# Blank matmuls before the first values, and an earlier turn of the second batch's z, in a gated attention unit followed by a feed-forward layer

## The chip, the cores and the metric

The kernel runs on one core of one Trainium2 chip. A core has TensorE (PE) for matmuls, VectorE (DVE) and ScalarE (ACT) for elementwise work on what TensorE leaves, GpSimd (POOL) and SyncE (SP). In this kernel SP only issues transfers, in the order of its list; POOL does elementwise work and issues transfers too. The metric is the time of one execution in microseconds on the device, as the median of several runs.

## The reference

Eight batches of 3008 rows. For each batch the scores are z times z transposed, divided by 3008, negative ones set to 0, and squared; they weigh the rows of v, and the result is multiplied elementwise by u. All 24064 rows then go through a feed-forward layer of 2048 hidden values with the gate h * sigmoid(1.702 h).

```python
batch, seq, d_model = (8, 3008, 256); d_qk = 64
scores = (1.0 / S) * np.matmul(z, z.transpose(0, 2, 1))
attn = np.maximum(scores, 0.0) ** 2
x = (u * np.matmul(attn, v)).reshape(B * S, D)
h = x @ w_in                       # 256 -> 2048
g = h * (1.0 / (1.0 + np.exp(-1.702 * h)))
out = g @ w_out                    # 2048 -> 256
```

## The kernel before

**Units.** The rows of a batch are cut into six units of 512 rows (the last is shorter). Unit n is batch n // 6, part n % 6. `scores` computes z times z transposed for a pair of 128-row tiles against the 512 rows of a unit: two matmuls (L263), a relu that leaves the PSUM tile `sc` (ACT, L292, or DVE, L294), and a square in place (ACT L278 or DVE L280). The squares are kept in a ring of 14 tiles `ap_`, or, for units 0 and 1, in memory lent from buffers that the second batch needs only later: the second value buffer V16[1], the second turned z, ZT[1], and z16. Since scores are symmetric, from unit 3 on part of the squares are not computed again but taken transposed by a transfer (L242, tiles `T`).

**Values.** `values` multiplies squares with v (L403; L465 for the last half tile) into four PSUM banks, two for each half h of a unit. `both_sums` moves two banks to a tile `sums` (ACT L382, DVE L384), POOL adds its halves (L377) and multiplies by u (L419) into X. X is transposed by SP (L318, XT), and its row halves are swapped into XS (L336). There are three `sums` buffers, shared with the second layer: the one for the last half of unit 4 is the one that held the first output half of block 0 until its store (L548).

**Feed-forward.** `hidden` computes two groups of 128 hidden values for a block of 512 rows (L493), ACT the sigmoid (L500), DVE the product (L504); `outs` multiplies by w_out (L531) into the same PSUM banks as the values. The block of unit n is worked three units later.

**Order.** The whole program is laid out by a planner at build time: it keeps a clock `now` for each engine with estimated costs, and a list `work` of value and output steps that TensorE takes in order. When a step isn't ready, or a PSUM tile for `sc` or `hg` is free, `filler` may put in a score pair or a hidden group, whichever is more urgent by its due place in `work`. Elementwise work goes to the engine that the planner has free first; SP's transfers are sorted by due unit. The order on each engine is fixed by this, and at run time each engine goes through its own list and waits on semaphores.

**Side steps.** Loads of later data hang on certain places of `work`: `at(n, j, f)` runs f when TensorE's list comes to value tile j of unit n. Each first calls `hold`, a POOL copy of two elements of the newest square, so that POOL (and so the transfers behind it) waits until the program has come that far. For each batch b these places issue `load_z` (POOL, three transfers into z16), `turn_z` (POOL copies z next to itself, L118, then SP transposes all of z16 into ZT, L119, 24 blocks of 128), and four quarters of v (`load_v`, POOL). The first scores of the next batch need ZT; they come in the fifth unit of the batch before.

**Start.** z of batch 0 is loaded in four parts, cast, and turned by TensorE itself (`turn_q`, L634), while eight matmuls on a blank tile run ahead of it (L625). Then come the first scores; the values (L403) begin when the first squares are there.

Of the kernel before, what the change touches and what calls it, by code (L numbers as in the profile page):

```python
# [8 lines left out]
F32 = mybir.dt.float32  # L9
F16 = mybir.dt.float16  # L10
P = 128
# [3 lines left out]
def kernel(  # L15
# [13 lines left out]
    B, S, D = u.shape  # L29
# [15 lines left out]
    LAG = 3  # L45
    RING = (LAG + 1) * TB
    H = P // 2
# [5 lines left out]
    dve, act, pe, sp, pool = nc.vector, nc.scalar, nc.tensor, nc.sync, nc.gpsimd  # L53
# [7 lines left out]
    psB = ctx.enter_context(tc.tile_pool(name="psB", bufs=1, space=bass.MemoryType.PSUM))  # L61
# [21 lines left out]
    def rows(b, dram, lo, hi, dst, eng, twice=2):  # L83

        full = min(hi, NF)
        if full > lo:
            eng.dma_start(  # L87
                dst[:, :full - lo, :],
                dram[b, lo * P:full * P].rearrange("(n p) d -> p n d", p=P),
            )  # L90
        if hi > NF:
            for h in range(twice):
                eng.dma_start(dst[h * SREM:(h + 1) * SREM, NF - lo, :], dram[b, NF * P:S].unsqueeze(1))
# [4 lines left out]
    def load_v(b, q):  # L98
        rows(b, v, q * VN, (q + 1) * VN, V16[b % 2][:, q * VN:(q + 1) * VN, :], pool)
# [5 lines left out]
    def load_z(b):  # L105
        rows(b, z, 0, NJ, z16[:, :, 0, :], pool)
# [9 lines left out]
    def turn_z(b):  # L116
        turned.add(b)
        pool.tensor_copy(z16[:, :, 1, :], z16[:, :, 0, :])  # L118
        sp.dma_start_transpose(ZT[b % 2], z16.rearrange("p n a d -> p (n a d)"))  # L119
# [8 lines left out]
    T_SC, T_SW, T_MM, T_HG = 0.215, 0.1, 0.107, 0.215  # L128
    T_LAT, T_SEM, T_DMA = 0.25, 0.1, 3.5
    now = {"pe": 6.0, "act": 6.0, "dve": 7.0, "pool": 6.0, "sp": 6.0}  # L130
# [21 lines left out]
    def advance(t):  # L152

        while ops:
            best = None
            for o in ops:
                e = min(o[3], key=lambda x: max(now[x], o[0]) + cost[(x, o[2])])
                key = (max(now[e], o[0]), o[2] not in FIRST, o[2] == "sq", o[1])
                if best is None or key < best[0]:
                    best = key, o, e  # L160
            (start, *_), o, e = best
            if start > t:
                break
            ops.remove(o)
            now[e] = start + cost[(e, o[2])]
            o[4](e, now[e] + T_SEM)
        while now["sp"] <= t:
            can = [o for o in sends if o[0] <= t and (o[4] is None or o[4]())]
            if not can:
                break  # L170
            o = min(can, key=lambda o: (o[2], o[0]))
            sends.remove(o)
            now["sp"] = max(now["sp"], o[0]) + cost[("sp", o[1])]
            o[3](now["sp"])

    def pe_at(rows_, dur):
        if mode[0] != rows_:
            now["pe"] += T_SW
            mode[0] = rows_
        now["pe"] += dur  # L180
        return now["pe"] + T_LAT
# [39 lines left out]
    def hold():  # L221

        pool.tensor_copy(scrap, latest[0][:1, 0, :2])
# [140 lines left out]
    def half(x, g):  # L364
        return x[g * H:(g + 1) * H]
# [94 lines left out]
    def halves(n):  # L460

        V = V16[n // NIS % 2]
        for q in range(NIB // 2):
            for g in range(2):
                pe.matmul(  # L465
                    Os[(n, g)][g][:, q, :], half(squares_of(n, NJ - 1, 2 * g + q), g), half(V[:, NJ - 1, :], g),
                    start=False, stop=False,
                )
        pe_at(H, 2 * T_MM)
        drop(n, NJ - 1)  # L470
# [15 lines left out]
    def hidden(m, fg):  # L486
        p_ = take_ps()
        hg = psA.tile([P, 2, TB], F32, name="hg", tag="A")
        p0 = (m * TB) % RING
        for c in range(2 * NK):  # L490
            for e in range(2):
                x = XT if c % 2 == e else XS
                pe.matmul(  # L493
                    hg[:, e, :], half(W1[:, fg // 2, c, fg % 2 * P:(fg % 2 + 1) * P], e), half(x[:, c // 2, p0:p0 + TB], e),
                    start=(c == 0), stop=(c == 2 * NK - 1),
                )

        def sig(e, at):
            tsg = pb.tile([P, 2, TB], F16, name="tsg", tag="tsg")
            act.activation(tsg, hg, AF.Sigmoid, scale=1.702 / FSC)  # L500

            def gt(e, at):
                GT = pb.tile([P, 2, TB], F16, name="GT", tag="GT", bufs=NG)
                dve.tensor_tensor(GT, hg, tsg, ALU.mult)  # L504
                GTs[(m, fg)] = (GT, at)
                set_ps(p_, at)

            push(at, "gt", ("dve",), gt)

        push(pe_at(H, 4 * T_HG), "sig", ("act",), sig)  # L510
# [45 lines left out]
    work = []  # L556
    EDGE, TAIL, NFIRST, NLAST = 6, 9, 4, 4
    for n in range(NTB + LAG):
        m = n - LAG
# [33 lines left out]
    def at(n, j, *fns):  # L593
        def go():
            hold()
            for f in fns:
                f()
        side[(n, j)] = go
# [4 lines left out]
    for b in range(1, B):  # L603
        n0 = (b - 1) * NIS
        late = b == 1
        at(n0 + 1 + 2 * late, 13, lambda b=b: load_z(b))
        at(n0 + 2 + 2 * late, 13, lambda b=b: turn_z(b))
        for q in range(VQ):
            at(n0 + 3 + late + q // 2, (EDGE, 12)[q % 2], lambda b=b, q=q: load_v(b, q))


    NZ = NJ // 4
# [8 lines left out]
    blank = pap.tile([P, 2, ISUP], F16, name="blank", tag="ap_")  # L621
# [9 lines left out]
    def turn_q(q):  # L631
        ztps.append(psB.tile([P, NZ, P], F16, name="ztp", tag=f"B{q % 2}{q // 2}"))
        for jj in range(NZ):
            pe.transpose(ztps[q][:, jj, :], z16[:, q * NZ + jj, :, :].rearrange("p a d -> p (a d)"), ident)  # L634

    def keep_q(q):
        dve.tensor_copy(ZT[0][:, q * NZ:(q + 1) * NZ, :], ztps[q])
# [10 lines left out]
    cast_z(3)  # L648
    keep_q(2)
    turn_q(3)  # L650
    now["pe"] = 8.0
    advance(7.0)
    keep_q(3)

    def ready_of(w):

        if w[0] in "ors":
            at = [squares_at(w[1], j) for j in w[2]] + [v_at[w[2][-1] // VN] if w[1] < NIS else 0.0] + ([bank[w[3]]] if w[0] == "o" and w[2][0] == 0 else [])
        else:
            at = [GTs.get((w[1], w[2]), (None, None))[1]] + ([bank[w[3]]] if w[2] == 0 else [])  # L660
        return None if None in at else max(at)

    def urgent(key, lead):
        return before[due[key]] - before[wi] - lead

    def filler():

        p_ = ps_free[ps_next % 2]
        if p_ is None or p_ > now["pe"]:
            return None  # L670
        can = []
        if nxt < len(pairs) and pairs[nxt][0] // NIS in turned and min(now["act"], now["dve"]) < now["pe"] + 0.8:
            old = len(ring) - NA
            if pairs[nxt] in home or old < 0 or not a_left[ring[old]]:
                can.append((urgent(("a",) + pairs[nxt], 3.0), "a"))
        if hnext < len(hids) and hnext - outs_done < NG and now["act"] < now["pe"] + 1.5 and now["dve"] < now["pe"] + 2.0:
            m = hids[hnext][0]
            xt = xt_at[m * TB // 64:(m + 1) * TB // 64]
            if None not in xt and max(xt) <= now["pe"]:
                can.append((urgent(("h",) + hids[hnext], 5.0), "h"))  # L680
        return min(can, default=None)

    wi = 0
    while wi < len(work):
        advance(now["pe"])
        w = work[wi]
        r = ready_of(w)
        late = r is None or r > now["pe"]
        f = filler()
        if f:  # L690
            if f[1] == "a":
                scores(1)
            else:
                hidden(*hids[hnext])
                hnext += 1
            continue
        if late:
            step = min([t for t in [r, ps_free[ps_next % 2]] + [o[0] for o in ops + sends] + [now[e] for e in ("act", "dve", "pool", "sp")] if t is not None and t > now["pe"]], default=now["pe"] + 0.1)
            now["pe"] = step
            assert now["pe"] < 2000.0  # L700
            continue
        if w[0] == "o":
            key = (w[1], w[2][0])
            if key in side and w[3] == 0:
                side.pop(key)()
            values(*w[1:])
        elif w[0] == "r":
            halves(w[1])
        elif w[0] == "s":
            shorts(w[1])  # L710
        else:
            outs(*w[1:])
        wi += 1
# [34 lines left out]
```

## Time and profile before

| what | us |
|---|---|
| time, median of 3 runs (lowest, highest) | 1249.58 (1248.88, 1251.04) |
| the profiled execution's own time | 1251.23 |
| its span | 1249.33 |
| TensorE busy | 1228.6 |
| DVE busy | 937.6 |
| ACT busy | 819.1 |
| POOL busy | 472.5 |
| HBM read, written | 60.29 MB, 24.64 MB |

The span is the part of an execution between the first and the last instruction that the profiler records; the profiled execution's own time is 1.90 us longer than it. Mean granted clock of TensorE over the span: 0.996 of full speed. Lines of the kernel are given as L and a number; `out<-in` names the tile written and the tiles read. A wait is given with what ended it. The chain is followed back from the last instruction to whatever released each step.

### The profile page before, as it was taken

How to read it: one execution, taken by the hardware profiler on the slowest of the kernel's cores; microseconds unless marked ns; L12 is line 12 of the kernel's file. 1: busy time of each engine (PE TensorE's matmuls, PEld its weight loads, DVE VectorE, ACT ScalarE, POOL GpSimd, SP SyncE). 2: the span in 40 equal slices, each digit the busy share in tenths (PEclk: the TensorE clock that was granted, in tenths of full speed). 3: DMA queues.
4: the chain of work that ended last, by engine and by line, in shares of the span. 5: the costliest groups of instructions: out<-in, count | busy, mean ns of one | idle time of the engine just before them, and what ended most of it. 6: DMA issues, size and time to landing. Idle time of an engine off the chain costs nothing.

```text
span 1249.3 us, 41891 instructions
## 1 busy us (share of the span) xinstructions
PE 1228.6 (98%) x18584; PEld 1011.8 (81%) x18584; DVE 937.6 (75%) x906; ACT 819.1 (66%) x933; POOL 472.5 (38%) x447
## 2 busy tenths in 40 slices
PE   8998999999999999999999999999999999999998
PEld 5876789988998877888778887788877888778886
DVE  7975877777888778876788768877688776877556
ACT  7855676666767657766577656676566765766444
POOL 5443334332433324343343424343343434332331
PEclk8999999999999999999999999999999999999999
DMA  9997887766986939889398684969759877574211
GB/s 151 172 166 153 145 138 131 133 132 123 133 149 135 154 91 143 142 138 165 77 142 155 128 147 90 139 125 166 131 105 141 161 127 119 112 137 110 67 45 60
DMA packets 442135, 161.74 MB, mean 129 GB/s; under 512 B 351841, under 2 KB 441953, under 8 KB 441953
## 3 DMA queue, kind: packets, MB, share of 16 engines
q1 hardware_dynamic: 390528, 141.62, 59.0%
q0 software_dynamic: 51424, 17.44, 13.8%
q8 instruction: 145, 2.38, 0.8%
q14 instruction: 38, 0.30, 0.1%
HBM read 60.29 MB, written 24.64 MB: 68 GB/s over the span
## 4 chain that ended last, share of the span: by engine, by line
PE 93%; DVE 5%; issue 1%; DMA 0%; ACT 0%; DVEq 0%; ACTq 0%
PE O L403 36%; PE hg L493 25%; PE yps L531 24%; PE sc L263 6%; PE O L478 1%; DVE GT L504 1%; PE O L465 1%; DMA ZT<-z 0%; PE warm L625 0%; DVE sums L384 0%; PE ztp L634 0%; DVE ap__8041 L280 0%; DVE ap__2880 L280 0%; DVE ap__713 L280 0%; DVE ap__18581 L280 0%
## 5 line engine op out<-in xcount | busy, mean ns | idle before, releaser
L504 DVE TENSOR_TENSOR GT<-hg,tsg 128x1024 f16<-128x1024 f32 x376 | 456.7, 1220 | 211.1 <-ACT tsg L500 209.9
L500 ACT ACTIVATE tsg<-hg 128x1024 f16<-128x1024 f32 x376 | 380.9, 1023 | 274.8 <-PE hg L493 248.2
L377 POOL TENSOR_TENSOR sums<-sums 128x512 f32<-128x512 f32 x188 | 249.0, 1325 | 666.4 <-ACT sums L382 349.4
L493 PE MATMUL hg<-XT,W 64*128 64x512 f16 x1504 | 387.9, 376 | 3.0 <-DVE GT L504 1.9
L531 PE MATMUL yps<-W,GT 64*128 64x256 f16 x6016 | 374.2, 270 | 1.3 <-DVE GT L504 0.9
L493 PE MATMUL hg<-XS,W 64*128 64x512 f16 x1504 | 370.3, 376 | 0.0
L531 PEld LDWEIGHTS <-GT 64*128 64x128 f16 x6016 | 324.1, 94 | 47.5 <-DVE GT L504 1.4
L493 PEld LDWEIGHTS <-W 64*128 64x128 f16 x3008 | 175.9, 94 | 87.5 <-issue 6.1
L403 PE MATMUL O<-V,T 64*128 64x256 f16 x3392 | 217.4, 269 | 0.1
L403 PEld LDWEIGHTS <-T 64*128 64x128 f16 x3392 | 185.9, 94 | 28.1 <-issue 0.3
L419 POOL TENSOR_TENSOR X<-sums,RU 128x512 f16<-128x512 f32 (+2 forms) x104 | 140.6, 1353 | 7.8
L263 PE MATMUL sc<-ZT 64*128 64x512 f16 x688 | 126.6, 380 | 10.7 <-DMA ZT<-z 4.5
L382 ACT ACTIVATE sums<-O 128x512 f32<-128x512 f32 x114 | 65.2, 596 | 52.8 <-PE O L403 47.1
L384 DVE TENSOR_SCALAR sums<-O 128x512 f32<-128x512 f32 x78 | 52.9, 687 | 33.9 <-PE O L403 30.1
L382 ACT ACTIVATE sums<-yps 128x512 f32<-128x512 f32 x111 | 63.8, 592 | 17.1 <-PE yps L531 15.9
L384 DVE TENSOR_SCALAR sums<-yps 128x512 f32<-128x512 f32 x73 | 50.0, 685 | 14.1 <-issue 9.9
L263 PEld LDWEIGHTS <-ZT 64*128 64x128 f16 x688 | 40.1, 95 | 17.8 <-issue 7.6
L87 POOL DMA_DIRECT2D V<-in_v_dram x32 | 28.0, 878 | 0.0
L87 POOL DMA_DIRECT2D z<-in_z_dram x7 | 10.9, 1564 | 0.4 <-PE hg L493 0.4
L478 PE MATMUL O<-V,T 128*64 128x256 f16 x160 | 10.3, 275 | 0.0
L118 POOL COPY z<-z 128x1536 f16<-128x1536 f16 x7 | 10.2, 1452 | 0.0
L478 PEld LDWEIGHTS <-T 128*64 128x64 f16 x160 | 8.1, 110 | 1.9 <-issue 1.9
(1536 smaller groups left out, 1522.2 us busy)
## 6 DMA issues: line engine op xcount, KB each, us to landing
out_dram<-sums SPq DMA_DIRECT2D x92, 256.0 KB, 4.0
RU<-in_u_dram SPq DMA_DIRECT2D x40, 512.0 KB, 4.5
V<-in_v_dram POOLq DMA_DIRECT2D x24, 384.0 KB, 7.2
XS<-XT SPq DMA_DIRECT2D x60, 128.0 KB, 4.0
RU<-in_u_dram SPq DMA_DIRECT2D x8, 384.0 KB, 3.7
z<-in_z_dram POOLq DMA_DIRECT2D x7, 368.0 KB, 9.4
V<-in_v_dram POOLq DMA_DIRECT2D x8, 320.0 KB, 9.1
XT<-X SPq DMA_TRANSPOSE x144, 2.5
```

Source lines behind the costliest of these rows:

```text
L87: eng.dma_start(dst[:, :full - lo, :], dram[b, lo * P:full * P].rearrange("(n p) d -> p n d", p=P),)
L263: pe.matmul(sc[:, g, :], Z[h0:h0 + DQK, 2 * t + g, :], Z[h0:h0 + DQK, isup * NIB:(isup + 1) * NIB, :], start=True, stop=True,)
L377: pool.tensor_tensor(s_[:, 0, :, :], s_[:, 0, :, :], s_[:, 1, :, :], ALU.add)
L382: act.activation(s_[:, g, :, :], ps[g], AF.Copy, scale=scale)
L384: dve.tensor_scalar(s_[:, g, :, :], ps[g], scale, None, ALU.mult)
L403: pe.matmul(O[g][:, i2, :], half(sq, g), half(V[:, j, :], g), start=(j == 0 and i2 == 0), stop=(ends and j == js[-1] and (i2 == 1 or short)),)
L419: pool.tensor_tensor(X[:p, :, ib:ib + k, :].rearrange("p c n d -> p n c d"), both[:p, ib - 2 * h:ib - 2 * h + k, :].rearrange("p n (c d) - ...
L478: pe.matmul(O[c0:c0 + SREM, 1, :], squares_of(n, j, NIB - 1)[:, :SREM], V[:, j, :], start=False, stop=False, tile_position=(0, c0),)
L493: pe.matmul(hg[:, e, :], half(W1[:, fg // 2, c, fg % 2 * P:(fg % 2 + 1) * P], e), half(x[:, c // 2, p0:p0 + TB], e), start=(c == 0), stop= ...
L500: act.activation(tsg, hg, AF.Sigmoid, scale=1.702 / FSC)
L504: dve.tensor_tensor(GT, hg, tsg, ALU.mult)
L531: pe.matmul(Y[g][:, i2, :], half(GT[:, e, s * P:(s + 1) * P], g), half(W2[:, ff, :], g), start=(fg == 0 and e == 0 and i2 == 0), stop=(end ...
```

## The change

Three things are edited. First, while the planner has not yet placed the first value step (`wi == 0`) and finds TensorE waiting, it puts in matmuls of 64 rows by 256 columns on the blank tile, into a PSUM tile `idle` that nothing reads. Second, for the second batch alone, `load_z` hangs on value tile 8 of the fourth unit instead of 13, `turn_z` on tile 0 of the fifth unit instead of 13, and the first `load_v` of each pair on tile 7 instead of 6. Third, `filler` gets a condition for the hidden groups of block 0.

```diff
-        at(n0 + 1 + 2 * late, 13, lambda b=b: load_z(b))
-        at(n0 + 2 + 2 * late, 13, lambda b=b: turn_z(b))
+        at(n0 + 1 + 2 * late, 8 if late else 13, lambda b=b: load_z(b))
+        at(n0 + 2 + 2 * late, 0 if late else 13, lambda b=b: turn_z(b))
         for q in range(VQ):
-            at(n0 + 3 + late + q // 2, (EDGE, 12)[q % 2], lambda b=b, q=q: load_v(b, q))
+            at(n0 + 3 + late + q // 2, (EDGE + late, 12)[q % 2], lambda b=b, q=q: load_v(b, q))
...
     turn_q(3)
+    idle = psB.tile([P, D], F32, name="idle", tag="B00")
     now["pe"] = 8.0
...
-            if None not in xt and max(xt) <= now["pe"]:
+            if None not in xt and max(xt) <= now["pe"] and (m or work[wi][1] >= LAG or work[wi][0] == "y"):
                 can.append((urgent(("h",) + hids[hnext], 5.0), "h"))
...
             step = min([t for t in [r, ps_free[ps_next % 2]] + [o[0] for o in ops + sends] + [now[e] for e in ("act", "dve", "pool", "sp")] if t is not None and t > now["pe"]], default=now["pe"] + 0.1)
+            if wi == 0 and step - now["pe"] > 0.08:
+
+                pe.matmul(idle, half(blank[:, 0, :P], 0), half(blank[:, 0, :D], 0), start=True, stop=True)
+                pe_at(H, T_MM)
+                continue
             now["pe"] = step
```

In the lists of instructions that the two programs give, TensorE's differs by 16 blank matmuls with their weight loads, and DVE's and ACT's are the same. On POOL the doubling copy of z (L118) with its `hold` stands ahead of two quarter loads of v instead of behind them, and the `hold` ahead of the z load names an earlier square. On SP the transpose into ZT (L119) stands ahead of two stores (L548) and two swaps (L336) instead of behind them, directly behind the transpose of the square that the trace of before calls ap__1501.

## The prediction

> **What bounds the kernel now.** I read the page first (shares, chain), then TensorE's waits, then the stretches around the two largest waits, then SP's timeline. On the page:
>
> ```profile
> PE 1228.6 (98%) x18584; PEld 1011.8 (81%) x18584; DVE 937.6 (75%) x906; ACT 819.1 (66%) x933; POOL 472.5 (38%) x447
> PE 93%; DVE 5%; issue 1%; DMA 0%; ACT 0%; DVEq 0%; ACTq 0%
> ```
>
> TensorE is busy 98% of the span and carries 93% of the chain. Its instruction list after the change is the old one with 16 matmuls added, so time can be won only where TensorE waits or runs slowly. Its waits (us in total, times, longest):
>
> ```profile
> PE sc L263 <- DMA ZT<-z: 4.5, 1, 4.5
> ...
> PE sc L263 <- DVE ap__181 L294: 1.1, 1, 1.1
> ...
> PE sc L263 <- DVE ap__150 L294: 0.9, 1, 0.9
> ...
> PE sc L263 <- ACT ap__176 L292: 0.3, 1, 0.3
> ```
>
> One wait of 4.5 us stands out: scores that need the second batch's turned z. The other three lie at the start. Stretches (bounds, length, busy time of PE, PEld, DVE, ACT, POOL; then granted clock, DMA share, GB/s):
>
> ```profile
> 7.00:10.00 3.00, 1.69 (x18) 0.99 (x17) 2.41 (x5) 2.96 (x4) 2.57 (x4) 1.00 1.17 145
> 10.00:11.00 1.00, 0.39 (x2) 0.10 (x2) 1.00 (x2) 0.98 (x1) 0.00 (x0) 0.77 1.45 196
> 11.00:14.00 3.00, 2.45 (x20) 1.72 (x21) 2.97 (x4) 2.19 (x3) 0.00 (x0) 0.50 1.45 195
> 14.00:17.00 3.00, 3.00 (x28) 2.28 (x26) 0.59 (x2) 2.08 (x2) 0.00 (x0) 0.50 0.84 114
> 17.00:18.00 1.00, 1.00 (x18) 0.90 (x15) 1.00 (x1) 0.00 (x0) 0.00 (x0) 0.82 0.22 45
> 44.67:48.08 3.41, 1.94 (x34) 1.65 (x31) 3.41 (x3) 3.35 (x4) 3.33 (x3) 1.00 1.27 245
> 106.00:107.00 1.00, 0.79 (x6) 0.42 (x8) 0.14 (x1) 0.00 (x0) 0.00 (x0) 0.56 0.00 0
> 107.00:109.00 2.00, 2.00 (x24) 1.37 (x20) 1.68 (x2) 1.54 (x2) 0.07 (x1) 0.50 0.00 0
> 109.00:110.00 1.00, 1.00 (x12) 0.59 (x10) 0.01 (x1) 0.00 (x0) 1.00 (x2) 0.74 0.08 16
> ```
>
> The clock falls to 0.50 twice. Where a stretch mixes 1.00 and 0.50, its mean gives the switch: 0.77 in 10 to 11 puts the fall at 10.54; 0.82 puts the rise at 17.36; 0.56 and 0.74 give 106.12 and 109.52. So half speed lasted 6.82 and 3.40 us, once after thin work, once after the 4.5 us wait. 44.67 to 48.08 shows a stretch 57% busy after which the clock held.
>
> SP's timeline says why the turned z was late (start, us):
>
> ```profile
> 93.36 3.72 SPq L242 DMA_TRANSPOSE T<-ap__1501  x1
> 97.19 1.43 SPq L548 DMA_DIRECT2D out_dram<-sums  x2
> 98.73 1.49 SPq L336 DMA_DIRECT2D XS<-XT  x2
> 100.45 4.27 SPq L119 DMA_TRANSPOSE ZT<-z  x1
> ```
>
> SP issues without a break here; the turn stands behind two stores and two swaps. It lands 5.7 us after its issue began (the DMA view), at 106.15; TensorE had come to its scores at 101.71.
>
> **The change, part by part.** The sum is made against the profiled execution: 1251.23 us, span 1249.33 and 1.90 around it.
>
> *Blank matmuls.* The built list has 16: one, ten, three and two, each group behind a score pair between 8.04 and the first values. Full-clock work in the chain (start, us), and the DVE row in the slow stretch:
>
> ```profile
> 20.22 0.22 PE sc L263 x2
> 20.43 0.87 PE O L403 x16
> ```
> ```profile
> 16.89 1.22 DVE L294 TENSOR_SCALAR V<-sc 128x1024 f16<-128x1024 f32 x1 [2.41 <-PE sc L263]
> ```
>
> A blank has the O matmul's size, 64 rows by 256 columns: 0.87 / 16 = 0.054 us at least; 0.109 if a pair there ran side by side; 0.203 with its 64x128 weight load (94 ns in the groups) not hidden. I take 0.109, as all blanks use the same half. The ten follow the pair of 9.36 (issued by 9.57), end at 10.66 and push the pair of 10.04 to there. Nothing waits for that: its relu on DVE began at 11.41, behind another relu. At 0.203 the ten end at 11.60, DVE is 0.5 late, and the gain below shrinks by 0.5. The three lie in the wait that ended at 11.55. The two go ahead of the values: 11.55 + 0.22 + 0.22 = 11.99, against 11.93 now at half clock. So they cost nothing, behind waits of 0.9, 0.3 and 1.1 us.
>
> What they buy, if the clock holds: from there to the first values from ap__181 lie 48 O matmuls and two score pairs, 3 x 0.87 + 2 x 0.22 = 3.05 us, so 15.04; the trace has them at 17.64. Gain 2.6. DVE and ACT can follow: DVE idled 2.41 before 16.89, ACT 0.61 and 1.71. Their squares for the fourth to sixth groups (12.59, 13.72, 14.48) are ready before 15.0, 16.4 and 17.2. Value loads left the queue by 15.8, and the fourth quarter is first read near 20. Behind that, DVE, SP and the weight loads are all started by TensorE's progress, so they move with it.
>
> Does the clock hold? Counting issue time (0.22 a score pair, 0.06 a transpose, by 12 in a row of 0.87 with its latency), the 3.41 us before 10.54 had 12 transposes and three pairs, 1.4 us or 40%, and it fell; at 57% (44.67) it held. With ten blanks for the third pair the same stretch has 2.2 us, 65%. If a blank with half the rows counts half it is 49%, between the rows. I take that it holds, since one count lies above the row that held and the other in the middle; bounds of the gain 0 and 2.6.
>
> By the Trainium skill, "TensorE: Matmul & The Clock Gate", Part 1, half speed is the state after about one idle window of some 3.4 us, and the windows run free of the kernel. The 3.40 and 6.82 us here, one and two times 3.41, agree with such windows; that it fell after one with three score pairs in it does not agree with "idle". By that rule alone any blank would hold it, and the sum stays as it is.
>
> *z loaded at value 8 instead of 13.* On POOL it now waits for the square of ap__1085 (done 62.95) instead of ap__1134 (64.68). The load began at 65.36 and took 10.8 us to land; the copy that reads it began only at 89.51. Two microseconds earlier changes nothing; its 2.65 us of POOL issue lie in an idle stretch up to 74.20. Worth 0.
>
> *z turned with the first tiles.* On POOL the doubling copy (1.45 us) moves ahead of two V loads: it starts at 87.55, ends at 89.0, and the loads start 1.45 late. Unit 6 reads them first, some 60 us on: cost 0 there. On SP the turn moves ahead of two stores and two swaps and starts behind T<-ap__1501, at 97.19. It lands 5.7 later at 102.9, and TensorE waits 102.9 - 101.7 = 1.2, with the restart 1.3. Gain 3.2. Bounds: the V loads now press later on the transposes before it (7.2 us to land against 2.5 for the page's XT<-X), so the turn may start 1 us later or take 1 more; or 0.7 sooner. Wait 0.6 to 3.3.
>
> A wait of 1.3 leaves 62% of any 3.41 us busy, above the 57% that held, so the second slow stretch goes: 3.40 / 2 less 0.1 before work began = 1.6.
>
> What is late next: the stores go out at 101.56 instead of 97.19, and land by their row's 4.3 us at 105.9, by the fastest of the next ones (2.8) at 104.4. Their sums buffer is the one that ACT and DVE fill for the last value half of unit 4, at 107.33 and 108.00 now. In their lists both wait for that store, with squares and relus queued behind, and TensorE's second output half needs the bank that they empty. TensorE, from 103.0, reaches that after 0.22 + 0.22 + 1.31 + 0.44 + 0.44 = 2.6, at 105.6; the bank is free 0.8 after the landing, 105.2 to 106.7. Cost 0 to 1.1, taken 0.4. The swaps land near 108.5; their reader in TensorE's list comes 440 matmuls later (over 24 us). The XT<-X behind them waits for POOL's gate anyway. The third edit of the planner (hidden layers of the first block) moves no instruction.
>
> Sum: -2.6 - 3.2 - 1.6 + 0.4 = -7.0, so 1251.23 - 7.0 = 1244.2. The profiled execution is 1.65 over the median shown. One step of 3.41 us at half speed costs 1.7, so other executions may have had one step fewer; the changed kernel should have none of either, so I keep 1244.2 for its median, and 1249.58 - 7.0 = 1242.6 is the other end.
>
> **Rivals.**
> (1) The clock falls at the start all the same: blanks leave gaps (0.8 us before 9.36) and use half the rows. For it: 49% is not far from 40%. Against: 65% by time. Then -7.0 + 2.6 = -4.4, 1246.8. The same page of the Trainium skill, "A second HAM failure mode: psum-queue depth-cycling", describes micro-idling between matmul groups enough to drop the clock, which speaks for this rival.
> (2) The turn stays late: the V loads, moved behind the copy, hold up T<-ap__1501 and the turn by 2 us. For it: that transpose took 3.72 to issue against 1.24 for a free one. Against: the swaps and stores are out of the way. The wait is 3.3, the clock falls after it: -7.0 + 2.0 + 1.6 = -3.4, 1247.8. Both together: -0.8, 1250.4.
> (3) Slower, by the store: ACT and DVE stand at the late store, TensorE at the bank. At a landing like the z load's (10.8) the second store, out at 102.3, lands at 113.1, the bank is free at 113.9: 8.3 us of waiting, and half speed after it. -2.6 - 3.2 + 8.3 = +2.5, 1253.7. It decides from a landing near 110.6 (a wait of 5.8); the stores' own rows are 2.8 to 4.3, which speaks against.
>
> **How the numbers follow.** Forecast 0.58, (1) 0.20, (2) 0.14, both 0.04, (3) 0.04. The range 1242.0 to 1248.2 takes in the median's end with the bank's 0.4 not spent, (1), and (2) with 0.4 more; it leaves out some 0.13. A measurement here tells 0.2%, 2.5 us, from no change. Faster is under 1247.1: the forecast, most of (1), a part of (2): 0.77. Same 0.18: the rest of these, and both together. Slower 0.05.
>
> **What would show it.** Clock 1.00 from 8 to 120; the values from ap__181 near 15.0; the turn in SP's timeline right behind T<-ap__1501; TensorE's wait for ZT near 1.3; ACT's sums of unit 4 waiting for a store by about 2. Wrong: a clock of 0.50 after 10, a wait for ZT of 3 or more, or a new wait of TensorE for sums of over 1 us.

## The result, and the profile after

| | before | after |
|---|---|---|
| median of 20 executions each, us | 1250.36 | 1247.67 |
| lowest, highest | 1248.77, 1251.58 | 1244.19, 1249.53 |
| profiled execution, its span | 1251.23, 1249.33 | 1249.53, 1247.8 |

The ratio is 0.998, interval 0.9973 to 0.9987: about 2.5 us faster, and just at the 0.2% that can be told from no change. The forecast was 7.0 us against the profiled execution of before, or 5.4 between the medians (1249.58 to 1244.2); a little over a third of the first came, and less than half of the second. The time lies inside the range given. The executions of the changed kernel spread over 5.3 us, and the profiled one is the longest of the 20. They go by TensorE's mean clock: the five at 1.000 took 1244.19 to 1246.32 us, the eleven at 0.998 or 0.999 took 1247.41 to 1248.68, and the four at 0.996, like the profiled one, 1249.39 to 1249.53.

The page after (busy times, then the shares of the chain by engine):

```profile
PE 1228.2 (98%) x18600; PEld 1012.1 (81%) x18600; DVE 937.7 (75%) x906; ACT 819.2 (66%) x933; POOL 472.9 (38%) x447
PE 93%; DVE 5%; DMA 1%; issue 1%; ACT 0%; DVEq 0%; ACTq 0%
```

The 16 blanks are there and the shares are as before, with transfers now 1% of the chain. TensorE's waits after:

```profile
PE sc L263 <- DMA ZT<-z: 4.3, 1, 4.3
...
PE sc L263 <- DVE ap__150 L294: 0.6, 1, 0.6
...
PE sc L263 <- ACT ap__146 L292: 0.3, 1, 0.3
...
PE sc L263 <- DVE ap__183 L294: 0.2, 1, 0.2
```

The three small waits at the start shrank where the blanks now stand: 1.1 became 0.2 (the last row), 0.9 became 0.6, and the 0.3 for ap__176 is gone; the 0.3 of the list is another wait, ahead of the first blank. The wait for ZT stayed: 4.3 against 4.5. Timelines show what happened to each of the two parts (start us, us). TensorE's, one row of before and then two of after:

```profile
17.64 0.40 PE L403 MATMUL O<-V,ap__181 64*128 64x256 f16 x4
```
```profile
11.82 1.05 PE L403 MATMUL O<-V,ap__146 64*128 64x256 f16 x16
...
14.87 0.40 PE L403 MATMUL O<-V,ap__183 64*128 64x256 f16 x4
```

SP's after:

```profile
87.51 1.38 SPq L242 DMA_TRANSPOSE T<-ap__1475  x1
89.01 3.69 SPq L242 DMA_TRANSPOSE T<-ap__1518  x1
93.35 8.11 SPq L119 DMA_TRANSPOSE ZT<-z  x1
101.52 1.08 SPq L548 DMA_DIRECT2D out_dram<-sums  x2
```

At the start the values of the fourth score group come at 14.87 instead of 17.64. In SP's list the turn is now where the diff says, right behind the transpose of ap__1518 (the ap__1501 of before). But issuing it took 8.11 us instead of 4.27. The DMA view of the same stretch (count, KB each, us from issue to landing) shows why:

```profile
V<-in_v_dram POOLq DMA_DIRECT2D x2, 384.0 KB, 9.1
...
T<-ap__1475 SPq DMA_TRANSPOSE x1, 11.3
T<-ap__1518 SPq DMA_TRANSPOSE x1, 11.9
ZT<-z SPq DMA_TRANSPOSE x1, 10.1
```

The same row of before:

```profile
ZT<-z SPq DMA_TRANSPOSE x1, 5.7
```

Before, the two transposes ahead of the turn landed in 7.3 and 7.2 us, and the loads were through at 97.25, ahead of the turn at 100.45. Now all three share the transfer engines with the two quarter loads of v, the later of which lands at 99.67, and all are slow. Two stretches of the same execution show the price (length, busy of PE, PEld, DVE, ACT, POOL, clock, DMA share, GB/s):

```profile
96.00:99.00 3.00, 3.00 (x57) 2.79 (x52) 2.90 (x3) 1.86 (x3) 0.00 (x0) 1.00 1.38 86
101.00:103.00 2.00, 0.00 (x0) 0.00 (x0) 0.00 (x0) 0.00 (x0) 0.64 (x1) 0.71 1.28 293
```

With the last of the v loads among them the engines are as busy (1.38) but move 86 GB/s; when the rest of the turn runs almost alone they move 293. (A share over 1 means that packets on one engine overlap.) The clock is in the second line too: it fell at 101.8, and the next three stretches show when it came back.

```profile
101.00:102.00 1.00, 0.00 (x0) 0.00 (x0) 0.00 (x0) 0.00 (x0) 0.64 (x1) 0.92 1.28 290
102.00:108.00 6.00, 4.51 (x38) 2.69 (x40) 2.26 (x3) 1.55 (x3) 1.71 (x3) 0.50 0.63 180
108.00:109.00 1.00, 1.00 (x16) 0.76 (x14) 1.00 (x2) 1.00 (x2) 0.93 (x1) 0.66 0.00 0
```

By the means, half speed lasted from 101.84 to 108.68: 6.8 us, where before it lasted 3.4. So in this execution the start gained 2.8 and the stretch behind it, with the turn, lost 1.0 (the table below).

**A ruler.** Every profile of this study can be cut at the same two matmuls of TensorE's list, whose order never changes: the first with the fourth score group (start 17.64 before) and the 1001st of the output matmuls, L531 (273.96 before). From there to the end of the span the fourteen profiles of before, after and the experiments lie between 974.9 and 975.6 us, so what an edit does is in the two stretches ahead of it (us):

| kernel | to the 4th group | from there to the 1001st output matmul |
|---|---|---|
| before | 17.64 | 256.3 |
| after | 14.87 | 257.3 |
| e1 blanks only | 15.22 | 257.9 |
| e2 z only | 14.40 | 255.2 |
| e3, e9 v loads late | 14.50, 14.79 | 250.3, 250.3 |
| e4 the same, old turn | 14.96 | 251.1 |
| e5, e10 v loads late, no blanks | 15.93, 14.95 | 250.3, 250.3 |
| e6 v loads late alone | 15.78 | 254.7 |
| e7 all v loads early | 14.61 | 260.7 |
| e8 turn in two parts | 14.57 | 256.4 |
| e11 half the blanks | 16.23 | 249.7 |
| e12 e8 with four sums buffers | 14.88 | 251.9 |

### The profile page after: what moved, and what is told of

It is laid out like the page before. It is cut to its first block, busy times and chain, and to the rows that moved or that the text cites. A ratio compares the mean times of both kernels' runs of the same rounds, so it can differ in the third digit from the quotient of the medians.

```text
span 1247.8 us, 41921 instructions
## 1 busy us (share of the span) xinstructions
PE 1228.2 (98%) x18600; PEld 1012.1 (81%) x18600; DVE 937.7 (75%) x906; ACT 819.2 (66%) x933; POOL 472.9 (38%) x447
## 4 chain that ended last, share of the span: by engine, by line
PE 93%; DVE 5%; DMA 1%; issue 1%; ACT 0%; DVEq 0%; ACTq 0%
PE O L403 36%; PE hg L493 25%; PE yps L531 25%; PE sc L263 6%; PE O L478 1%; DMA ZT<-z 1%; PE O L465 1%; DVE GT L504 1%; PE warm L625 0%; DVE sums L384 0%; DVE ap__8058 L280 0%; DVE ap__2897 L280 0%; PE ztp L634 0%; DVE ap__1020 L280 0%; DVE ap__1039 L280 0%
## 5 line engine op out<-in xcount | busy, mean ns | idle before, releaser
L531 PE MATMUL yps<-W,GT 64*128 64x256 f16 x6016 | 374.7, 270 | 1.2 <-DVE GT L504 0.9
L531 PEld LDWEIGHTS <-GT 64*128 64x128 f16 x6016 | 324.5, 94 | 47.9 <-issue 1.5
L384 DVE TENSOR_SCALAR sums<-yps 128x512 f32<-128x512 f32 x73 | 50.0, 685 | 14.1 <-issue 9.9
L118 POOL COPY z<-z 128x1536 f16<-128x1536 f16 x7 | 10.2, 1454 | 0.0
```

Of the source, the lines that this page charges most:

```text
L384: dve.tensor_scalar(s_[:, g, :, :], ps[g], scale, None, ALU.mult)
L531: pe.matmul(Y[g][:, i2, :], half(GT[:, e, s * P:(s + 1) * P], g), half(W2[:, ff, :], g), start=(fg == 0 and e == 0 and i2 == 0), stop=(end ...
```

## The experiments

Ratios are to the kernel of before on the same chip, with 95% intervals.

### One part at a time

e1 takes the z places of before and keeps the blanks; e2 does the reverse.

```diff
 e1
-        at(n0 + 1 + 2 * late, 8 if late else 13, lambda b=b: load_z(b))
-        at(n0 + 2 + 2 * late, 0 if late else 13, lambda b=b: turn_z(b))
+        at(n0 + 1 + 2 * late, 13, lambda b=b: load_z(b))
+        at(n0 + 2 + 2 * late, 13, lambda b=b: turn_z(b))
...
-            at(n0 + 3 + late + q // 2, (EDGE + late, 12)[q % 2], lambda b=b, q=q: load_v(b, q))
+            at(n0 + 3 + late + q // 2, (EDGE, 12)[q % 2], lambda b=b, q=q: load_v(b, q))
 e2
-                pe.matmul(idle, half(blank[:, 0, :P], 0), half(blank[:, 0, :D], 0), start=True, stop=True)
-                pe_at(H, T_MM)
-                continue
```

> The blank matmuls with the second batch's z loaded, copied and turned where it was before. If the whole gain of the change is the start (the values from the fourth score group came at 14.87 against 17.64), this is as fast as the changed kernel or within 1 us of it: about 2.5 us faster than before, and TensorE waits 4 to 5 us for ZT as before. If the earlier turn gave part of the gain (wait shorter, or less time at half clock after it), this loses that part and is 1.5 us or more slower than the changed kernel.

> The z load, copy and turn in their new places, without the blank matmuls. Same question from the other side: about the time of before (within 0.5 us) if the earlier turn gives nothing, with a wait for ZT of 4 us or more and the turn taking 8 us to issue; 3 us or more faster than before if the turn is worth what was forecast. The clock should fall in the first 20 us as before.

Measured: e1 1249.54 us, ratio 0.9994 (0.9986 to 1.0003), a wait for ZT of 5.1. e2 1247.92 us, 0.9978 (0.9968 to 0.9988), a wait of 3.3 and a turn that took 4.6 us to issue. The first reading of the two profiles (the start gained all, the turn nothing) is wrong for the mean: the z part alone gives the whole gain, the blanks alone can't be told from nothing. Two things were behind this. In e2, without blanks, the clock did not fall in the first 20 us at all, and the fourth group came at 14.40: the 6.8 us of half speed at the start of the profiled execution of before is one case among several. And the loads were paid for at another place. SP's timeline and the DMA view of e2:

```profile
90.07 4.58 SPq L242 DMA_TRANSPOSE T<-ap__1501  x1
95.31 4.64 SPq L119 DMA_TRANSPOSE ZT<-z  x1
```
```profile
T<-ap__1501 SPq DMA_TRANSPOSE x1, 9.3
ZT<-z SPq DMA_TRANSPOSE x1, 6.6
```

The later v load, issued at 87.09, landed 8.66 us on, at 95.75. So the turn, begun at 95.31, had it beside it for 0.4 us only and took 4.64 us to issue; in after it began at 93.35 and had a load beside it for 6.3 us. In e2 it was the two transposes ahead that had the loads beside them, and the turn began late. It landed at 101.94, against 103.45 in after.

### The v loads

e3 is the changed kernel with the second batch's v loads a unit later. e4 is e3 with z at the old places; e6 is e4 without blanks, that is, the kernel of before with nothing but late v loads; e5 is e3 without blanks. On POOL two loads move behind the sums work; no other list changes.

```diff
-            at(n0 + 3 + late + q // 2, (EDGE + late, 12)[q % 2], lambda b=b, q=q: load_v(b, q))
+            at(*((5, (6, 9, 12, 14)[q]) if late else (n0 + 3 + q // 2, (EDGE, 12)[q % 2])), lambda b=b, q=q: load_v(b, q))
```

> The changed kernel with the two quarter loads of v that stood behind the copy of z moved a unit later, after the turn; nothing else is moved on any engine. Theory A, that the turn and the two transposes ahead of it are slow because these loads move at the same time: the turn issues in 4.3 us or less and lands 6 us or less after it is begun, TensorE waits for ZT 1.3 us or less, the clock stays at full speed, and the time is 1241 to 1244 us. Rival B, that the turn is slow because it comes right behind two other transposes in SP's queue, whatever POOL loads: it still takes 8 us to issue and 10 to land, the wait stays near 4.3, and the time is 1247 to 1248 us.

> The same move of the v loads, but z is loaded, copied and turned at the old places (blank matmuls kept). Theory A: SP's queue runs faster without the loads, so that the turn starts earlier even behind the stores and swaps; the wait for ZT falls to between 0 and 2.5 us, and the time is 1242 to 1245.5 us: the loads alone are worth most of it. Rival B: the turn takes 4.3 us to issue as before and begins at the same place against TensorE, the wait stays at 4 to 4.5 us, 1247 to 1248 us.

> The kernel of before with nothing but the v loads moved a unit later: no blank matmuls, z at the old places. If the loads alone are what delays the turn (theory A), the wait for ZT falls to under 1.5 us here too and the time is 1244 to 1246.5 us, 4 to 6 us faster than before; if they matter only when the turn is moved among them, it stays at 1249.5 to 1250.5 us.

Measured: e3 1242.46 us, 0.9934 (0.9922 to 0.9947); e4 1244.02, 0.9957 (0.9943 to 0.9971); e6 1246.41, 0.9968 (0.9955 to 0.9981). SP's timeline and the DMA view of e3:

```profile
88.06 1.39 SPq L242 DMA_TRANSPOSE T<-ap__1518  x1
90.11 3.67 SPq L119 DMA_TRANSPOSE ZT<-z  x1
```
```profile
T<-ap__1475 SPq DMA_TRANSPOSE x1, 3.8
T<-ap__1518 SPq DMA_TRANSPOSE x1, 4.1
ZT<-z SPq DMA_TRANSPOSE x1, 6.6
```

Without the loads the transpose ahead takes 1.39 us to issue instead of 3.69, the turn starts at 90.11 and takes 3.67; it lands at 96.7, before TensorE needs it, and no wait for ZT is left in e3's list. Theory A holds, rival B falls (the turn is still right behind two transposes). The turn itself took 6.6 us to land, a little over the 6 expected. e4 and e6 show that moving the loads is worth 4 to 5 us by the ratios even with the turn in its old place (0.9957 against e1's 0.9994, and 0.9968 against 1): waits of 0.6 and 2.5. e6 is the less certain of the two. Its time lies just inside the range expected, but its seven executions spread from 1242.69 to 1247.86, its median is only 2.9 us under that of before, and in its profile a wait of 2.5 was left where under 1.5 was expected.

### The load doubled

e7 puts all four quarter loads behind the copy of z: `(4, 7 + q)` in the same line.

> The changed kernel with all four quarter loads of v of the second batch behind the copy of z, instead of two: the suspected load doubled. Theory A: the turn is slowed further, it lands 2 to 5 us later against TensorE than in the changed kernel, the wait for ZT is 6 to 9 us, and the time is 1250 to 1253 us. Rival B (loads don't matter): the wait stays at 4 to 4.5 us and the time at 1247 to 1248 us. A middle case, that the two later loads queue behind the first two and only the first ones meet the transposes: up to 1 us more.

Measured: 1253.44 us, 1.0029 (1.0017 to 1.0041): slower than before. TensorE's wait and SP's turn in e7:

```profile
PE sc L263 <- DMA ZT<-z: 8.6, 1, 8.6
```
```profile
93.40 12.01 SPq L119 DMA_TRANSPOSE ZT<-z  x1
```

No loads (e3), two (after), four (e7): 3.67, 8.11 and 12.01 us to issue the same transpose, and 6.6, 10.1 and 14.1 to land it. Each row is one execution, and the number of loads alone does not decide: e2 has two as well, at 4.64 and 6.6, as they were nearly through when its turn began. The time, at 1253.4, is 0.4 over what was expected. By the Trainium skill, "DMA: Bandwidth & Descriptors", section "Queues, rings and completion order", an engine takes turns between the queues that have work for it, a packet each time; these three rows agree with transposes that get only their turn among the loads' packets. Turns alone do not give the size. In after from 96 to 99 the loads' queue had 0.227 of the engines' time and SP's 1.132, and yet the bytes of both together fell to 86 GB/s. SP's 645 packets, the transposes', took 84 ns each there, against 18 ns from 101 to 102 (1134 packets at 1.276) and 22 ns in e3 from 90.2 to 93.8 (2751 packets at 1.047). Why they are longer beside the loads, no run here shows.

### The turn in two parts, and the store behind it

```diff
-        sp.dma_start_transpose(ZT[b % 2], z16.rearrange("p n a d -> p (n a d)"))
+        for lo, hi in ((0, 8), (8, NJ)) if b == 1 else ((0, NJ),):
+            sp.dma_start_transpose(ZT[b % 2][:, lo:hi, :], z16[:, lo:hi, :, :].rearrange("p n a d -> p (n a d)"))
```

> The changed kernel with its turn issued as two transposes, the first 8 of the 24 blocks and then the other 16. TensorE's first scores of the second batch need only the first six blocks. If the turn is slow because its packets trickle among the v loads, the first part lands when about a third is through: 3 to 5 us sooner, the wait for ZT falls to 0 to 1.5 us and the time is 1242.5 to 1245 us. If the turn only begins to move when the loads are done, the first part lands no more than 2 us sooner: 1245.5 to 1247 us.

Measured: 1247.21 us, 0.9981 (0.9972 to 0.9989), the time of the changed kernel, though the wait for ZT did fall to 1.2. Neither case of the expectation: the first part landed at 100.00, 3.4 us before the whole turn of after, but the gain was spent at once. Line numbers are one higher here. TensorE's longest waits, and who held the bank (ACT's and DVE's timelines):

```profile
PE yps L532 <- ACT sums L383: 2.8, 1, 2.8
...
PE sc L264 <- DMA ZT<-z: 1.2, 1, 1.2
```
```profile
105.02 0.60 ACT L383 ACTIVATE sums<-O 128x512 f32<-128x512 f32 x1 [5.07 <-DMA out_dram<-sums]
```
```profile
105.04 0.69 DVE L385 TENSOR_SCALAR sums<-O 128x512 f32<-128x512 f32 x1 [3.33 <-DMA out_dram<-sums]
```

ACT and DVE both stand until the store behind the turn has landed, since the sums buffer they fill is the one it reads; TensorE stands at the bank that they empty, and behind that wait the clock fell for 3.4 us, at 106.89. e12 gives them a fourth buffer (`bufs=4`), with no list changed.

> e8 (the turn in two transposes, v loads where the change put them) with four sums buffers instead of three; no engine's list changes otherwise. In e8 TensorE waited only 1.2 us for ZT, but 2.8 for the bank that ACT and DVE could not empty until the store behind the turn had landed. If that store is the whole of the second wait, it goes, the clock holds, and the time is 1243 to 1245 us, 2.5 to 4 us faster than e8's 1247.21. If something else in SP's queue holds the bank, the wait stays near 2.8 and the time at 1246.5 to 1248 us.

Measured: 1243.59 us, 0.9946 (0.9932 to 0.9959), four executions within 0.3 us, no wait for the bank, 1.5 for ZT, and no fall of the clock from the first score pairs to 1241 us. The store was the whole of the second wait.

### The blanks where nothing hides them

> The v loads a unit later and z in its new places (no wait for ZT is left: 1242.46 us with blank matmuls), but without the blank matmuls. Theory C, that the blanks save about 2 us at the start and that in the changed kernel this is spent at the wait for ZT, since the turn is bound by transfers and does not move with TensorE: now that the wait is gone, leaving the blanks out costs it in full, 1244 to 1245 us. Rival D, that the start of the profiled execution of before (6.8 us at half clock) was an unlucky one and that most executions lose little there: 1242.5 to 1243.5 us.

e5 measured 1242.0 us, 0.9938 (0.9925 to 0.995), as fast as e3. To compare the pair side by side, both were run again on one chip, with a third that drops every second blank.

> The kernel of e3 (blank matmuls, z in its new places, v loads a unit later) beside the next two on one chip, to price the blank matmuls where nothing at the wait for ZT can hide or eat their gain. From the profiles so far, the values from the fourth score group came at 14.5 to 15.2 us with blanks, and without at 14.4, 15.8, 15.9 or 17.6 as the clock fell in no, one or two windows; all that lies after keeps its distance. Theory (blanks hold the clock and are worth the difference of these means, 1.1 us): 1 us faster than the one without, with less spread. Rival D: within 0.5 us of it.

> The kernel of e5 (no blank matmuls) beside e9. Theory: slower than e9 by about 1 us, with mean clocks of 0.998 to 0.999 where e9 has 0.999 to 1.0. Rival D: within 0.5 us of e9.

> e9 with every second blank matmul left out: 8 in the same places. If the clock is held by the share of time with any matmul, 8 are too few in some phases and the time lies between e9 and e10; if the last ones only push the scores behind them back, it is 0.1 to 0.4 us faster than e9.

```diff
 e11
+                blanks += 1
+                if blanks % 2:
-                pe.matmul(idle, half(blank[:, 0, :P], 0), half(blank[:, 0, :D], 0), start=True, stop=True)
+                    pe.matmul(idle, half(blank[:, 0, :P], 0), half(blank[:, 0, :D], 0), start=True, stop=True)
```

Measured: e9 1242.42 (1241.65 to 1242.84), ratio 0.9936 (0.9922 to 0.9949); e10 1242.75 (1242.05 to 1244.74), 0.9942 (0.993 to 0.9955); e11 1242.19 (1241.4 to 1243.29), 0.9935 (0.9923 to 0.9948). The medians are within 0.6 us and the intervals cover each other, so rival D stands for the median; the one without blanks has the longest executions, up to 2 us over e9's. In e11's profile the clock fell at 11.1 for 3.4 us although 7 of the 8 blanks had run in the 3.4 us ahead of it: eight don't hold it in every execution, so not any blank will do. In none of the eight profiles with all 16 did it fall in the first 20 us; in the five without, it fell in three. The count is small, but the records of the clock in the traces add to it. In all fourteen, every stretch between two steps of the clock is a whole number of 3.413 us, so each execution has a beat, and one can count back to its first tick after the start of the span. Without blanks the clock fell where that tick came at 0.30, 0.91 or 1.67 us (before, e6, e5), and held where it came at 0.16 or 2.56 (e10, e2). With the 16 it held at 0.54, 1.07 and 1.49 too (e3, e8, e7), which lie between the three where it fell without them. That speaks for the blanks; whether they hold it in every execution stays open.

The fastest kernels here are those with the turn and the v loads moved (e3, e5, e9, e10, e11), at 0.9934 to 0.9942 of before. With or without blanks, their intervals cover each other.

## Why the prediction was wrong, point by point

- **Fast or slow.** Faster was right, though barely: by the prediction's own mark, 1247.1, the 1247.67 would be no change, but that mark was put from 1249.58, and the 20 executions of before gave 1250.36. The size was not right: 7.0 forecast, about 2.5 measured. By the single-part runs the blanks were worth 0.3 to 0.7 us (e9 against e10, e1 against before; neither can be told from nothing) for 2.6 in the sum, and the z part 1.8 to 2.7 for 4.4 (3.2 and 1.6 less 0.4), so both halves of the sum fell short by about 2.
- **The turn (term -3.2).** This is the step that failed: "It lands 5.7 later at 102.9, and TensorE waits 102.9 - 101.7 = 1.2." The row of 5.7 us came from a turn that ran when the v loads were done. Moved forward by two stores and two swaps, it ran into them, and took 10.1. The bound given ("may start 1 us later or take 1 more") was too narrow: e7, after and e3 show 14.1, 10.1 and 6.6 with four, two and no loads. TensorE's wait came out at 4.3 for the 1.2 of this step (3.3 in e2). With e1 against after and before against e2 the z part is worth 1.4 and 2.2 parts in a thousand, 1.8 to 2.7 us, with the clock's share in it.
- **"Unit 6 reads them first, some 60 us on: cost 0 there."** True of the readers, and beside the point. The loads cost where they run, not where they are read: 0.9980 became 0.9934 in e3, 5.7 us, by moving them.
- **The second slow stretch (term -1.6).** It hung on a wait of 1.3 and went the other way in the profiled execution, 6.8 us of half speed for 3.4. Its condition was sound: in the profiles with a wait for ZT of 1.5 or less (e3, e4, e5, e8, e9 to e12) the clock held through it, and in those with 2.5 or more (before, after, e1, e2, e6, e7) it fell.
- **The blanks (term -2.6).** In the profiled execution the place and the mechanism came out as forecast: the fourth group came at 14.87, forecast 15.04, and the clock held. The size was that of one execution. Without blanks the group came at 14.40, 14.95, 15.78, 15.93 and 17.64 in five profiles, mean 15.7; with 16 it lies at 14.50 to 15.22, mean 14.8. Beside each other the medians of e9 and e10 differ by 0.3 us. A blank itself cost what was taken: in after, eight in a row took 1.03 us and a single one 0.27, so each further one 0.109. Taking the row of one execution for the typical one was the mistake here; the 1.65 us between that execution and the median said so, and was explained as one step of half speed, but not carried into this term.
- **What moves with TensorE.** "DVE, SP and the weight loads are all started by TensorE's progress, so they move with it" held for TensorE and DVE up to the feed-forward layer (the first hidden layer starts at 55.98 in after, 58.51 before), but not quite for SP: in e1 TensorE reaches the wait 2.2 us sooner and the turn starts 1.65 sooner (98.80 against 100.45), so the wait grew to 5.1 and half speed behind it doubled. Most of what the blanks had won in that execution was given back there.
- **The store (term +0.4, and rival 3).** No cost in after: while TensorE stood at ZT, the store landed in 2.7 us. The wait was real all the same: 2.8 us in e8, as soon as the wait for ZT was short, and gone with a fourth buffer. The sum had its place, its engines and its order right.
- **Rival 2** is nearest to what happened: the loads made the turn late. The place was another: the transpose ahead took 3.69 us to issue, as before (3.72), and it was the turn itself that took 4.4 us longer to land. Its 1247.8 is close to 1247.67 partly by luck, since it kept 2.6 for the blanks and took 2.0 for the delay.
- **z loaded sooner.** It began at 61.09 here and its copy ran at 85.02, still long after the load had landed (71.6); no run tried it alone.

## What to carry to other kernels

How long a transfer took here depended on what else was moving. Before one is moved in a queue, look up what the other queues will be moving at the new time, and price it by a row measured among such traffic. A load that nobody needs soon belongs after one that somebody is waiting for, even when it goes through another queue. And when the clock or a wait takes steps from one execution to the next, one profile's stretch is a sample; price it by several before it becomes a term of a sum.

## What was not expected of the hardware

- Transposes slow down by far more than the load's bytes: in after, at a transfer share of 1.38 the engines moved 86 GB/s with both kinds of traffic, and at 1.28 they moved 293 GB/s with the turn nearly alone. The 293 is the best case: other stretches without loads moved 226 GB/s (before, 102.5 to 105.5, share 1.22) and 165 GB/s (e3, 90 to 96, 1.15).
- The clock falls after stretches that are far from idle (three score pairs and twelve transposes in 3.41 us, 40% by issue time), and whether it does changes from one execution of the same code to the next: e5 and e10 are one kernel, and it fell at 11.91 in e5 and not at the start of e10. No share of work that decides can be read from these traces. By the profile's own busy time the stretch that fell, 7.13 to 10.54 of before, is as busy as the one that held, 44.67 to 48.08 (1.95 and 1.94 us of 3.41). And in e10 the clock held after a window of the beat, 6.98 to 10.40, with the same twelve transposes and three pairs and only the end of one more pair. Its steps keep a beat of their own: from the first rise to the second fall it is 88.75 us both before (17.36 to 106.11) and in e6 (14.56 to 103.31), 26 times 3.413 us, though TensorE's waits lay elsewhere. The Trainium skill, "TensorE: Matmul & The Clock Gate", Part 1, says that the windows run free of the kernel; these rows agree.
